# Spectrum and product buffer of a long-convolution kernel: four channels next to each other per frequency instead of two

## The chip, the cores and the metric

The kernel runs on one core of one Trainium2 chip. The metric is the time of one execution on the device, in microseconds (us); the time shown for a kernel is the median of its runs. Names of engines in the profile: PE is TensorE (matmuls), PEld its weight loads, DVE is VectorE, ACT is ScalarE, POOL is GpSimd, SP issues the DMAs. L90 is a line of a helper that records every operation, so nearly every row carries it and groups are told apart by their tiles.

## The reference

A long convolution per channel by FFT, and a gated projection behind it, for 8 batches of 6400 positions and 128 channels in fp32:

```python
def _attn_ref(x, h):                      # x: (8, 6400, 128), h: (6400, 128)
    L = 2 * S
    Yf = np.fft.rfft(x, n=L, axis=1) * np.fft.rfft(h, n=L, axis=0)[None]
    return np.fft.irfft(Yf, n=L, axis=1)[:, :S, :]

def _moe_ref(x, w_val, conv_w, w_out):    # x: what _attn_ref returned
    xp = np.concatenate([np.zeros((B, K - 1, D)), x], axis=1)
    gate_pre = sum(conv_w[k] * xp[:, k:k + S, :] for k in range(K))     # K = 5
    return (1 / (1 + np.exp(-gate_pre)) * (x @ w_val)) @ w_out
```

## The kernel before

The 6400 positions are laid out as N1 = 100 by N2 = 64, and the transforms are matmuls in steps. All data is fp32. The profile counts two PE instructions, and two weight loads, for each fp32 matmul of the code: a "pass" below is one of these two.

- **Forward step** (`Forward.group`): one group takes 8 channels. Four matmuls (weights: two channels of x, 128 columns; moving: the constants `r1_sb`, 200 columns) write a PSUM pair `pt`. Four copies bring it to the buffer `gy` (or to `gh`, a view of `dt`, for the filter h): 64 partitions by 400 elements each, on ACT in odd groups and on DVE in even groups.
- **Buffer `gy`**: per partition it holds, for each of the 128 channels, 100 frequencies. Before, the channels lie in pairs: `gy[p, d // 2, k, d % 2]`. Two channels of a pair are neighbours in memory (8 bytes together), the next frequency of the pair follows 8 bytes on, and the next pair 800 bytes on.
- **Second step** (`s2_mm`): for each frequency k one matmul with weights `m2_sb[:, k, :]` (128 dense columns) and, as moving operand, all 128 channels of that frequency, `src[:, :, k]`: 64 neighbouring pairs, 800 bytes apart. Eight frequencies fill a PSUM pair of two banks.
- **Product** (`Product`): the result is multiplied by the spectrum of h: `swap` (ACT, PSUM to `w_t`), `mul_u` (DVE, PSUM times `h_sb` into `gy`), `mul_t` (DVE, `w_t` times `h_sb`), `add` (POOL, into `gy`; DVE for the last block). `kdt` gives `w_t` and `h_sb` the same order of elements as `gy` has within a block of eight frequencies. `Spectrum` makes the spectrum of h once, at the start, and stores it to the scratch `hd` in device memory.
- **Third step** (`s3_quad`): for each channel one matmul with the channel's 100 frequencies as weights, `gy[:, d // 2, :, d % 2]` (100 columns, one every 8 bytes), and the constants `r3_sb` as moving operand (128 dense columns). Four channels fill one PSUM bank, which ACT or DVE copies to `dt`.
- **Fourth step and gates** (`Chunk`, `Gates`): `s4` (weights from `dt`, 128 dense columns; moving `m4_sb`, 100 columns), then taps, projection, sigmoid, gate, output projection, store.

The order of the work on every engine is the order of the code (`_InOrder`). Per batch there are two phases: first 16 rounds of two `s3_quad` and one `Forward.group` for the next batch (plus, from batch 1 on, the tail of the last batch's gates, `trail`); then the gates of this batch with the 13 `Product` blocks of the next batch between them. The first batch has a prologue in their place: 32 forward groups (16 for h, 16 for x), then spectrum and product blocks. The last batch has no forward groups and no products.

Of the kernel before, what the change touches and what calls it, by code (L numbers as in the profile page):

```python
# [9 lines left out]
F32 = mybir.dt.float32  # L10
# [5 lines left out]
C = 128  # L16
N1 = 100
N2 = 64
# [3 lines left out]
NKB = 13  # L22
TAPS = 5
XG = 8
NG = C // XG
NW = 2 * C + TAPS
SW = 256
# [75 lines left out]
def longconv_moe(ctx: ExitStack, tc: tile.TileContext, x, h, r1, m2, r3, m4, w64, out):  # L103
# [4 lines left out]
    cp = ctx.enter_context(tc.tile_pool(name="cp", bufs=1))  # L108
# [2 lines left out]
    psp = tc.tile_pool(name="psp", bufs=2, space=bass.MemoryType.PSUM)  # L111
    pairs = [ps2, psp.__enter__()]

    gy = cp.tile([128, C // 2, N1, 2], F32, name="gy")
    dt = cp.tile([128, N2 * 2 * C], F32, name="dt")
    dv = dt.rearrange("p (n c d) -> p n c d", c=2, d=C)
    gh = dt[:, : N1 * C].rearrange("p (d k t) -> p d k t", k=N1, t=2)
    m4_sb = cp.tile([PX, N2 + 1, N1], F32, name="m4_sb")
    r1_sb = cp.tile([N1, 2 * N1], F32, name="r1_sb")
    r3_sb = cp.tile([128, 2 * N2], F32, name="r3_sb")  # L120
# [5 lines left out]
    h_sb = [cp.tile([128, KB * C], F32, name=f"h_{i}") for i in range(HB)]  # L126
    x_sb = [cp.tile([PX, XG, N2], F32, name=f"x_{i}") for i in range(XB)]
    w_t = [cp.tile([128, KB * C], F32, name=f"w_{i}") for i in range(WB)]
# [66 lines left out]
    def pair():  # L195
        pairs.append(pairs.pop(0))
        return pairs[-1].tile([128, 2, 512], F32, name="pt2", tag="pt2")

    def single():
        return ps1.tile([128, 512], F32, name="pt1", tag="pt1")  # L200

    class Forward:
# [5 lines left out]
        def load(self, n=1):  # L208
            for _ in range(n):
                if self.n < NG:  # L210
                    nc.sync.dma_start(x_sb[self.n % XB], self.src[self.n])
                    self.n += 1

        def group(self):
            g = self.i
            self.i += 1
            t = x_sb[g % XB]
            pt = pair()
            for m in range(4):
                nc.tensor.matmul(  # L220
                    pt[:, m // 2, (m % 2) * SW : (m % 2) * SW + 2 * N1],
                    lhsT=t[:N1, 2 * m : 2 * m + 2, :].rearrange("p j n -> p (j n)"),
                    rhs=r1_sb,
                    start=True,
                    stop=True,
                )
            self.load()
            v = pt.rearrange("p b (m x) -> p b x m", x=SW)
            return [
                lambda e, j=j, c=c: e(  # L230
                    self.dst[c * N2 : (c + 1) * N2, 4 * g + 2 * j : 4 * g + 2 * j + 2],
                    v[j * N2 : (j + 1) * N2, :, c * N1 : (c + 1) * N1],
                )
                for j in range(2)
                for c in range(2)
            ]

    def count(kb):
        return min(KB, N1 - kb * KB)
# [6 lines left out]
    def h_load(kb):  # L246
        if kb < NKB:
            n = count(kb) * C
            for r in range(2):
                nc.sync.dma_start(h_sb[(2 * kb + r) % HB][:, :n], hd[kb, r, :, :n])  # L250
# [5 lines left out]

    def kdt(t, kb):
        n = count(kb)
        return t[:, : n * C].rearrange("p (d k t) -> p d k t", k=n, t=2)

    def s2_mm(src, kb):
        pt = pair()
        n = count(kb)
        for k in range(n):
            nc.tensor.matmul(
                pt[:, k // 4, (k % 4) * C : (k % 4 + 1) * C],
                lhsT=m2_sb[kb % M2B][:, k, :],
                rhs=src[:, :, kb * KB + k],
                start=True,
                stop=True,  # L270
            )
        if n <= 4:
            return pt[:, 0, : n * C].rearrange("p (k d t) -> p d k t", t=2, d=C // 2)
        return pt.rearrange("p b (k d t) -> p d (b k) t", t=2, d=C // 2)

    hx = h_sb + [dt[:, N1 * C + i * KB * C : N1 * C + (i + 1) * KB * C] for i in range(2)]

    class Spectrum:
        def __init__(self, kb):
            self.kb, self.v = kb, s2_mm(gh, kb)  # L280
            self.h = [hx[(2 * kb + r) % len(hx)] for r in range(2)]

        def real(self):
            t = kdt(self.h[0], self.kb)
            act(t[:N2], self.v[:N2])
            act(t[N2:], self.v[:N2])

        def imag(self):
            t = kdt(self.h[1], self.kb)
            dve(t[N2:], self.v[N2:])  # L290
            n = count(self.kb) * C
            nc.gpsimd.tensor_copy(self.h[1][:N2, :n], self.h[1][N2:, :n])
# [7 lines left out]
    class Product:  # L300
        def __init__(self, kb, h=None):
            self.kb, self.v = kb, s2_mm(gy, kb)
            self.t = kdt(w_t[kb % WB], kb)
            self.u = gy[:, :, kb * KB : kb * KB + count(kb)]
            self.h = [kdt(i, kb) for i in h or [h_sb[(2 * kb + r) % HB] for r in range(2)]]
# [15 lines left out]
    def s3_quad(d0):  # L321
        pt = single()
        for q in range(4):
            d = d0 + q
            nc.tensor.matmul(
                pt[:N1, q * 2 * N2 : (q + 1) * 2 * N2],
                lhsT=gy[:, d // 2, :, d % 2],
                rhs=r3_sb,
                start=True,
                stop=True,  # L330
            )
        o = dv[:N1, :, :, d0 : d0 + 4].rearrange("p n c d -> p (n c) d")
        return lambda e: e(o, pt[:N1].rearrange("p (d m) -> p m d", d=4))
# [129 lines left out]
    for f in (fh, fx):  # L463
        for g in range(NG):
            e = f.group()
            if f is fh and fh.n == NG:
                left = fx.n - (g + 1 - (NG - XB))
                if left < 0:
# [82 lines left out]
    for b in range(B):  # L551
# [5 lines left out]
        if nxt:  # L557
            for kb in range(M2B):
                m2_load(kb)
            for kb in range(2):  # L560
                h_load(kb)
        for g in range(NG):
            e = [s3_quad(8 * g), s3_quad(8 * g + 4)]
            f = fx.group() if nxt else []
            e[0](act)
            e[1](dve)
            for i in f:
                i(act if g % 2 else dve)
            if trail:
                trail.pop(0)()  # L570
            if b == 0:
                m4_load(4 * g, 4 * g + 4)
                if LATER + g < NKB:
                    h_double(LATER + g)
                next(wgen, None)
                next(wgen, None)
# [48 lines left out]
def _lay_x(v):  # L625
    b = v.shape[0]
    q = np.zeros((b, PX, C, N2), np.float32)
    q[:, :N1] = v.reshape(b, N1, N2, C).transpose(0, 1, 3, 2)
    q = q.reshape(b, PX, NG, 2, 4, N2).transpose(0, 2, 1, 4, 3, 5)
    return np.ascontiguousarray(q.reshape(b, NG, PX, XG, N2))  # L630

# [35 lines left out]
```

## Time and profile before

| | us |
|---|---|
| median of 3 runs (1089.99 to 1090.17) | 1090.0 |
| the profiled execution's own time | 1088.27 |
| span of the profiled execution, first to last instruction | 1086.5 |
| PE busy in the span | 1047.0 |
| DVE busy | 851.1 |
| ACT busy | 725.2 |
| POOL busy | 413.3 |

Busy time is a sum over phases with different limits, so the rows below are read by phase. The profiled execution's own time is 1.73 us below the median of the runs and 1.77 us above its span. A row of the timeline merges neighbouring instructions of one kind; its second number reaches to the end of the last one, and matmuls overlap, so the time that a run of matmuls takes from the engine is the start of the next row less the start of this one.

### The profile page before, as it was taken

To read this page: it belongs to the slowest core of one execution; us is meant where nothing else is said; L and a number is where in the kernel's file an instruction comes from. 1 tells how busy PE (TensorE), PEld (TensorE's weight loads), DVE (VectorE), ACT (ScalarE), POOL (GpSimd) and SP (SyncE) were. 2 spreads that over 40 slices of the span, in tenths; PEclk is the share of its full clock that TensorE was granted. 3 is DMA by queue.
4 is the path that set the end of the run, shared out by engine and by line. 5 is a ranking of instruction groups with operands and counts; after the bars stand their busy time and mean duration, and the time that the engine had idled before them with its cause. 6 is when DMAs were issued, how large, how long until landed. Compare 5 with 4: busy or idle time off the path is not lost.

```text
span 1086.5 us, 19537 instructions
## 1 busy us (share of the span) xinstructions
PE 1047.0 (96%) x7480; PEld 939.1 (86%) x7480; DVE 851.1 (78%) x1177; ACT 725.2 (67%) x1174; POOL 413.3 (38%) x219
## 2 busy tenths in 40 slices
PE   8997899999999999999999999999999999999997
PEld 8986899779988899878998799888998799987975
DVE  6789678987599857987589875998579885898375
ACT  5798348865588556875488656884578745885365
POOL 0079104840078202870058400881028600683032
PEclk9999899999999999999999999999999999999999
DMA  5697967975199734976279752997249761892012
GB/s 154 210 312 187 331 218 244 305 220 176 54 324 285 266 95 136 334 216 231 69 241 322 222 174 52 337 278 262 83 163 330 207 235 51 291 306 81 18 39 83
DMA packets 109130, 221.13 MB, mean 204 GB/s; under 512 B 45354, under 2 KB 53518, under 8 KB 108814
## 3 DMA queue, kind: packets, MB, share of 16 engines
q1 hardware_dynamic: 109038, 219.89, 63.1%
q8 instruction: 59, 0.97, 0.4%
q14 instruction: 33, 0.27, 0.1%
HBM read 184.47 MB, written 39.32 MB: 206 GB/s over the span
## 4 chain that ended last, share of the span: by engine, by line
PE 75%; ACT 13%; DVE 7%; DMA 2%; issue 2%; POOL 1%; POOLq 0%; SPq 0%; DVEq 0%; ACTq 0%
PE pt L90 75%; ACT w L90 6%; ACT dt L90 4%; DVE w L90 3%; DVE gl L90 2%; ACT p L90 2%; DMA x<-xl 1%; ACT h L90 1%; DVE gy L90 1%; DMA m<-m 1%; POOL gy L90 0%; DVE dt L90 0%; POOL dt L90 0%; ACT gl L90 0%; DMA x<-hl 0%
## 5 line engine op out<-in xcount | busy, mean ns | idle before, releaser
L90 PEld LDWEIGHTS pt<-m_sb,dt 100*128 100x128 f32 x2048 | 242.4, 192 | 43.4 <-issue 30.5
L90 PEld LDWEIGHTS pt<-r_sb,gy 128*100 128x100 f32 x2048 | 239.7, 172 | 31.8 <-issue 17.7
L90 ACT COPY dt<-pt 100x512 f32<-100x512 f32 (+3 forms) x280 | 163.4, 584 | 142.0 <-PE pt L90 140.5
L90 PE MATMUL pt<-r_sb,gy 128*100 128x128 f32 x2048 | 244.9, 274 | 10.5 <-DVE gy L90 10.5
L90 POOL TENSOR_TENSOR gy<-gy,w 128x1024 f32<-128x1024 f32 x96 | 228.5, 2380 | 58.2 <-DVE w L90 57.4
L90 PE MATMUL pt<-m_sb,dt 100*128 100x100 f32 x2048 | 243.7, 274 | 3.5 <-DVE dt L90 2.6
L90 PE MATMUL pt<-r_sb,x 100*128 100x200 f32 x1152 | 216.3, 335 | 6.1 <-DMA x<-hl 4.1
L90 PEld LDWEIGHTS pt<-gy,m 128*128 128x128 f32 x1600 | 194.5, 188 | 21.6 <-issue 9.9
L90 DVE COPY dt<-pt 100x512 f32<-100x512 f32 (+2 forms) x164 | 110.9, 679 | 120.3 <-PE pt L90 114.6
L90 PE MATMUL pt<-gy,m 128*128 128x128 f32 x1600 | 201.3, 278 | 1.1 <-DVE dt L90 1.1
L90 PEld LDWEIGHTS pt<-r_sb,x 100*128 100x128 f32 x1152 | 193.1, 192 | 6.7 <-issue 4.3
L90 ACT COPY gy<-pt 64x400 f32<-64x400 f32 x256 | 124.6, 487 | 100.9 <-PE pt L90 88.5
L90 DVE COPY gy<-pt 64x400 f32<-64x400 f32 x256 | 146.3, 571 | 37.6 <-PE pt L90 35.0
L90 POOL MEMSET dt<- 128x4 f32 x8 | 0.8, 106 | 456.9 <-PE pt L90 456.9
L90 DVE TENSOR_TENSOR w<-w,h 128x1024 f32<-128x1024 f32 (+1 forms) x100 | 150.4, 1504 | 0.0
L90 DVE SCALAR_TENSOR_TENSOR dt<-pt,w_sb,dt 128x500 f32<-128x500 f32 (+7 forms) x216 | 132.5, 629 | 12.7 <-POOL dt L90 6.1
L90 ACT ACTIVATE w<-pt 64x1024 f32<-64x1024 f32 (+1 forms) x104 | 102.8, 989 | 37.1 <-PE pt L90 35.6
L90 DVE TENSOR_TENSOR gy<-pt,h 128x1024 f32<-128x1024 f32 (+1 forms) x100 | 117.3, 1173 | 8.5 <-ACT w L90 4.9
L90 POOL TENSOR_TENSOR dt<-dt,p 128x500 f32<-128x500 f32 (+1 forms) x64 | 101.5, 1586 | 57.2 <-DVE dt L90 31.5
L90 PE MATMUL pt<-dt,w_sb 128*128 128x500 f32 (+2 forms) x240 | 114.0, 564 | 3.2 <-ACT dt L90 3.1
L90 DVE SCALAR_TENSOR_TENSOR gl<-pt,w_sb,gl 128x500 f32<-128x500 f32 (+3 forms) x119 | 73.9, 622 | 39.5 <-ACT gl L90 30.1
L90 ACT COPY w<-pt 64x1024 f32<-64x1024 f32 (+1 forms) x104 | 101.1, 972 | 1.5
(35 smaller groups left out, 722.7 us busy)
## 6 DMA issues: line engine op xcount, KB each, us to landing
h<-hd SPq DMA_DIRECT2D x168, 512.0 KB, 6.5
m<-m SPq DMA_DIRECT2D x96, 512.0 KB, 6.1
x<-xl SPq DMA_DIRECT2D x128, 224.0 KB, 3.4
out<-dt SPq DMA_DIRECT2D x56, 250.0 KB, 6.1
out<-yl SPq DMA_DIRECT2D x40, 250.0 KB, 2.8
hd<-h SPq DMA_DIRECT2D x8, 512.0 KB, 5.5
x<-hl SPq DMA_DIRECT2D x16, 224.0 KB, 2.6
hd<-hd SPq DMA_DIRECT2D x14, 256.0 KB, 5.2
```

Of the source, the lines that this page charges most:

```text
L90: return self._tc.keep_in_program_order(call(*args, **kwargs))
```

## The change

`TQ = 4` channels lie side by side per frequency in `gy` and `gh`, in the products' temporaries `w_t` and in the spectrum of h (`h_sb`, `hd`): `gy[p, d // 4, k, d % 4]`. Four channels are neighbours (16 bytes together), the next frequency of the four follows 16 bytes on, and the next four channels 1600 bytes on.

```diff
+TQ = 4
...
-    gy = cp.tile([128, C // 2, N1, 2], F32, name="gy")
+    gy = cp.tile([128, C // TQ, N1, TQ], F32, name="gy")
...
-    gh = dt[:, : N1 * C].rearrange("p (d k t) -> p d k t", k=N1, t=2)
+    gh = dt[:, : N1 * C].rearrange("p (d k t) -> p d k t", k=N1, t=TQ)
...
-                    self.dst[c * N2 : (c + 1) * N2, 4 * g + 2 * j : 4 * g + 2 * j + 2],
+                    self.dst[c * N2 : (c + 1) * N2, 2 * g + j].rearrange("p k (b m) -> p b k m", b=2),
                     v[j * N2 : (j + 1) * N2, :, c * N1 : (c + 1) * N1],
...
     def kdt(t, kb):
         n = count(kb)
-        return t[:, : n * C].rearrange("p (d k t) -> p d k t", k=n, t=2)
+        return t[:, : n * C].rearrange("p (d k t) -> p d k t", k=n, t=TQ)
...
         if n <= 4:
-            return pt[:, 0, : n * C].rearrange("p (k d t) -> p d k t", t=2, d=C // 2)
-        return pt.rearrange("p b (k d t) -> p d (b k) t", t=2, d=C // 2)
+            return pt[:, 0, : n * C].rearrange("p (k d t) -> p d k t", t=TQ, d=C // TQ)
+        return pt.rearrange("p b (k d t) -> p d (b k) t", t=TQ, d=C // TQ)
...
-                lhsT=gy[:, d // 2, :, d % 2],
+                lhsT=gy[:, d // TQ, :, d % TQ],
                 rhs=r3_sb,
```

No instruction is added, removed or moved on any engine, and the waits are the same; only the patterns of addresses differ. On DVE this shows at the end of the prologue's forward groups and at the first product. Before (64x400 is the copies' output of 64 partitions by 400 elements in one run, 128x64x16 that of `mul_u`):

```order
L90 COPY gy<-pt_401 64x400 x4
L90 COPY h_84<-pt_424 64x1024
L90 COPY h_86<-pt_433 64x1024
L90 TENSOR_TENSOR gy<-pt_448,h_83 128x64x16
L90 TENSOR_TENSOR w_91<-w_91,h_84 128x1024
```

The same rows of the changed kernel, whose lines stand one further down:

```order
L91 COPY gy<-pt_401 64x2x100x2 x4
L91 COPY h_84<-pt_424 64x1024
L91 COPY h_86<-pt_433 64x1024
L91 TENSOR_TENSOR gy<-pt_448,h_83 128x32x32
L91 TENSOR_TENSOR w_91<-w_91,h_84 128x1024
```

The copy into `gy` (and into `gh`) now writes pairs of elements, one pair every 16 bytes, where it wrote 400 elements in a row; `mul_u` and `add` touch `gy` in runs of 32 elements instead of 16; the other shapes stay.

## The prediction

> **What bounds the kernel now.** I read the page's engine shares and its chain first, then busy times by stage, then the chain of waits within one batch, then the timeline of PE for the pace of each kind of matmul.
>
> ```profile
> span 1086.5 us, 19537 instructions
> ...
> PE 1047.0 (96%) x7480; PEld 939.1 (86%) x7480; DVE 851.1 (78%) x1177; ACT 725.2 (67%) x1174; POOL 413.3 (38%) x219
> ...
> PE 75%; ACT 13%; DVE 7%; DMA 2%; issue 2%; POOL 1%; POOLq 0%; SPq 0%; DVEq 0%; ACTq 0%
> ```
>
> PE is busy 96% of the span and holds three quarters of the chain that ended last; ACT and DVE hold 20%. The windows tell where: the forward groups and the products of the prologue, then the two phases of the third batch.
>
> ```profile
> core 0: us, PE busy (x) PEld busy (x) DVE busy (x) ACT busy (x) POOL busy (x), PEclk, DMA share, GB/s
> 28.20:49.90 21.70, 21.70 (x128) 21.70 (x129) 17.85 (x32) 15.33 (x32) 0.00 (x0) 1.00 0.68 208
> 53.60:98.10 44.50, 41.23 (x346) 40.18 (x344) 40.82 (x31) 43.09 (x44) 37.02 (x19) 1.00 0.86 275
> ...
> 362.80:417.70 54.90, 54.77 (x398) 51.67 (x396) 37.19 (x60) 27.42 (x54) 0.00 (x0) 1.00 0.45 150
> 417.70:488.30 70.60, 69.77 (x498) 59.59 (x499) 63.32 (x79) 57.74 (x86) 49.30 (x25) 1.00 0.84 263
> ```
>
> In the third-step phase (362.8 to 417.7) PE is busy 54.77 of 54.90 us while DVE and ACT have 17.7 and 27.5 us to spare: PE alone is the limit there. In the gates phase PE is nearly as full, but there a busy PE is not always what is waited for. The chain of waits says where it is:
>
> ```profile
> 361.90 55.66 PE pt L90 x398
> 417.69 9.99 PE pt L90 x84
> 437.42 1.32 ACT dt L90 x4
> 441.83 1.65 ACT dt L90 x3
> 444.58 33.70 PE pt L90 x231
> 480.75 1.22 DVE w L90
> ```
>
> All of the third-step phase is PE (361.90 to 417.56). In the gates phase the first 9.99 us and 33.70 us from 444.58 on are PE's; between them ACT's copies and activations are the chain, and DVE takes the last 8 us.
>
> **What a pass costs PE.** The change alters how PE reads `gy` twice: as weights in the third step, as moving operand in the second. So I need the pace of each kind, from starts of neighbouring rows; the first row below is the group of the third step's weight loads, the others are of the timeline.
>
> ```profile
> L90 PEld LDWEIGHTS pt<-r_sb,gy 128*100 128x100 f32 x2048 | 239.7, 172 | 31.8 <-issue 17.7 <-POOL gy L90 10.6 <-DVE gl L90 1.4
> ...
> 118.25 1.91 PE L90 MATMUL pt<-r_sb,gy 128*100 128x128 f32 x16
> 120.00 1.52 PE L90 MATMUL pt<-r_sb,x 100*128 100x200 f32 x8
> 121.36 1.91 PE L90 MATMUL pt<-r_sb,gy 128*100 128x128 f32 x16
> ...
> 439.36 2.37 PE L90 MATMUL pt<-m_sb,dt 100*128 100x100 f32 x20
> 441.57 1.06 PE L90 MATMUL pt<-dt,w_sb 128*128 128x400 f32 x4
> ```
>
> A third-step pass takes (120.00 - 118.25) / 16 = 109.4 ns, a forward pass (121.36 - 120.00) / 8 = 170 ns, a fourth-step pass (441.57 - 439.36) / 20 = 110.5 ns. The first two move 128 and 200 dense columns: (170 - 109.4) / 72 = 0.84 ns a column and 2 ns beside it, so the moving columns set the pace, and the third step's 100 weights, one every 8 bytes, are loaded in its shade. The fourth step moves only 100 columns (86 ns by that rate) but loads 128 dense weights: there the load sets the pace, (110.5 - 2) / 128 = 0.85 ns a weight. Load and multiply run side by side, and the longer one counts. A load of 100 weights would take about 87 ns at that rate, so 22 ns of cover are left in a third-step pass.
>
> The second step:
>
> ```profile
> 55.47 2.02 PE L90 MATMUL pt<-dt,m 128*128 128x128 f32 x16
> 57.33 2.01 PE L90 MATMUL pt<-gy,m 128*128 128x128 f32 x16
> 59.18 2.01 PE L90 MATMUL pt<-dt,m 128*128 128x128 f32 x16
> ```
>
> (59.18 - 55.47) / 32 = 115.9 ns: 6.5 ns over the third step for the same 128 moving columns, 5.4 over the fourth step for the same 128 dense weights. What is special here is the moving operand: 64 pairs that lie 800 bytes apart. So a broken read costs PE something, and the two ways to write it down part ways for this change:
>
> - a **floor**: each new piece of memory takes at least 115.9 / 64 = 1.81 ns, however little of it is used;
> - a **charge**: each jump adds 6.5 / 64 = 0.10 ns.
>
> The third step's weights of today fit both, if a piece has at least 16 bytes: one weight every 8 bytes, two to a piece, 50 pieces of 1.81 ns are 91 ns, below 109.4.
>
> **The change part by part.**
>
> *Third step, weights.* Now one weight every 16 bytes: a piece of 16 bytes holds one. By the floor a load takes 100 x 1.81 = 181 ns, which is longer than the multiply, and the pace becomes 181 ns. By the charge it takes 87 + 100 x 0.10 = 97 ns, still hidden. No row of this trace has a PE read of one element per 16 bytes, so the price lies between: nothing (109.4 stays) and 181. I take 181: it comes from the only row in which PE reads broken data, and 16 bytes is the smallest piece that the rows allow; larger pieces (32 bytes) would again put two weights in each and cost nothing. By the Trainium skill (SBUF — State Buffer, Specifications) SBUF is read in lines of 16 bytes and at least two hits on a line are needed for full bandwidth. By that rule this change, which leaves one hit, slows the loads, and today's weights, with two, are just free; the trace agrees with the second half (109.4 ns), and no run here shows the first. [...]
>
> Sum: a round of the third-step phase has 16 third-step passes behind 8 forward passes. The load for a pass runs beside the pass before it. So the first load hides beside a forward pass (181 - 170 = 11 ns late) and 15 loads each make their pass 181 - 109.4 = 71.6 ns longer: 1.085 us a round. Seven batches of 16 rounds: 112 x 1.085 = 121.5 us. The last batch has no forward passes: 16 x 16 x 71.6 ns = 18.3 us. Together +139.8 us. All of it is on the path, by the chain of the phase above (55.66 us of PE without a break), and nothing else becomes late, since DVE and ACT had slack there already.
>
> *Second step, moving operand.* Now 32 pieces of 16 bytes: by the floor 58 ns, no limit any more. The pace falls to that of 128 dense weights, 110.5 ns: -5.4 ns a pass. What of it is on the path: in the gates phase those passes that lie in the two PE stretches of the chain.
>
> ```profile
> 419.63 3.95 PE L90 MATMUL pt<-gy,m 128*128 128x128 f32 x32
> ...
> 448.60 2.01 PE L90 MATMUL pt<-gy,m 128*128 128x128 f32 x16
> ...
> 477.40 1.08 PE L90 MATMUL pt<-gy,m 128*128 128x128 f32 x8
> ```
>
> The first stretch has 32 passes, the second five rows of 16 and one of 8 (first and last shown): 120 of the batch's 200. 7 x 120 x 5.4 ns = -4.5 us. The other 80 stand beside ACT's chain, and those of the prologue beside ACT too (43.09 of 44.50 us busy). At most, were all 1800 passes on the path, -9.7 us; at least 0, if the 6.5 ns come from loading and moving 128 columns at once and not from the jumps, a mixture that no row here has with a dense operand.
>
> *Copies of the forward groups.* They write pairs with a gap in place of one run.
>
> ```profile
> L90 DVE COPY gy<-pt 64x400 f32<-64x400 f32 x256 | 146.3, 571 | 37.6 <-PE pt L90 35.0
> L90 ACT COPY gy<-pt 64x400 f32<-64x400 f32 x256 | 124.6, 487 | 100.9 <-PE pt L90 88.5 <-DVE gl L90 10.1
> L90 DVE COPY dt<-pt 100x512 f32<-100x512 f32 x128 | 87.7, 689 | 109.5 <-PE pt L90 104.3 <-DMA m<-m 3.9
> ```
>
> The 512-element copy writes runs of four, 512 bytes apart, and costs (689 - 571) / 112 = 1.05 ns more per element, just as much as if both wrote dense runs. I take nothing for pairs, and a doubling (about 0.42 us a copy on DVE) as the other end. In the third-step phase even that hides (17.7 us to spare for 32 copies a batch on DVE, 13.4 us). In the prologue's forward groups DVE has four copies, 2.28 us, in two groups of PE, 2.71 us (16 passes of 170 ns): cover ends at 0.68 us a copy.
>
> *Products.* `mul_u`, `swap` and `add` keep their counts of elements, and their runs get longer.
>
> ```profile
> L90 POOL TENSOR_TENSOR gy<-gy,w 128x1024 f32<-128x1024 f32 x96 | 228.5, 2380 | 58.2 <-DVE w L90 57.4
> L90 DVE TENSOR_TENSOR gy<-pt,h 128x1024 f32<-128x1024 f32 x92 | 111.9, 1216 | 8.5 <-ACT w L90 4.9 <-DMA h<-hd 3.2
> L90 ACT COPY w<-pt 64x1024 f32<-64x1024 f32 x96 | 96.4, 1005 | 1.4
> ```
>
> Against the 400-element copies DVE's 1216 is (1216 - 571) / 624 = 1.03 ns an element, and ACT's 1005 is (1005 - 487) / 624 = 0.83: the rate of the other rows already, in spite of runs of two in PSUM. Nothing to win there, nothing to lose; POOL is far from the chain. The DMAs move the same blocks.
>
> *Sum.* +139.8 - 4.5 = +135.3 us. From the profiled execution's own 1088.27 us this is 1223.6; the median of the runs is 1.7 higher, so I say **1225 us**.
>
> **The rivals.**
>
> 1. *The weights' stride stays hidden* (a charge per jump, or pieces of 32 bytes). Speaks for it: the 22 ns of cover, and that the stride of 8 bytes is free today. It decides below a load of 109 ns, 1.07 ns a weight. Then only the second step is left: 1090 - 4.5 = 1085.5 us, between 1080 and 1090. The Trainium skill (SBUF — State Buffer, on cachelines) also says that fp32 may stride by 4 elements for free, which is this result if the stride of exactly 16 bytes is included; its own two-hits rule in the same passage says it is not. Chance 0.19, of it 0.15 for a gain over 0.2%.
> 2. *No effect at all*: weights hidden, and the 6.5 ns have nothing to do with the pairs. 1090 us. Chance 0.06.
> 3. *The copies become the bound of the prologue* while the weights stay hidden: at doubled copies, DVE needs 3.96 us per two groups against 2.71, 16 x 1.25 = +20 us, 1105 to 1110 us. Against it: dense and broken writes of the rows above run alike. Chance 0.02.
> 4. *A smaller price*: a load slower than its cover but below the floor. Each 10 ns over 109.4 give about 20 us: 1095 to 1195 us. Chance 0.06.
> 5. *A higher price*: the jump of one element costs more than that of a pair. At 2.6 ns a weight (half as much again as the floor) a pass takes 260 ns, +290 us, 1375. Nothing in the rows points there. Chance 0.04.
>
> **How the numbers follow.** The forecast with its own range of 1195 to 1245 us has 0.63: the low end is a load at twice the dense price, 2 x 0.85 x 100 = 170 ns, hence 112 x 15 x 60.6 + 256 x 60.6 ns = +117 us without and +113 with the second step's gain, 1203, and a little room; the high end is the floor plus 10 ns a pass. Cases of both signs hold much of the chance, so the range for 8 in 10 must reach to rival 1: 1083 to 1245 us. Left out are rival 5, the far end of rival 1 and some of the tails. A measurement of this kernel tells 0.2% (2.2 us) from no change: faster 0.15; same 0.10 (rival 2 and the rest of rival 1); slower 0.75.
>
> **What would show it.** In the changed kernel's timeline: third-step runs of 16 in about 2.85 us instead of 1.75, and their weight loads longer than the 172 ns of today by about 70; second-step runs of 16 in 1.77 instead of 1.85 us; third-step phases of 72 us instead of 55; copies of 571 and 487 ns as before. If third-step runs keep 1.75 us, the floor is wrong and rival 1 or 2 holds. If the runs lengthen but the phase does not, something else was the limit there.

## The result and the profile after

The changed kernel takes 1227.8 us (median of 4 runs, 1226.84 to 1228.37) against 1090.09 us before (1089.99 to 1093.09): ratio 1.1249, 95% interval 1.123 to 1.1268. The forecast was 1225.

The page of the changed kernel, the lines that answer to those of before:

```profile
span 1225.1 us, 19537 instructions
...
PE 1185.8 (97%) x7480; PEld 1085.8 (89%) x7480; DVE 852.7 (70%) x1177; ACT 733.5 (60%) x1174; POOL 412.5 (34%) x219
...
PE 82%; DVE 7%; ACT 7%; issue 2%; DMA 2%; POOL 0%; POOLq 0%; SPq 0%; DVEq 0%; ACTq 0%
```

The span grew by 138.6 us and PE's busy time by 138.8; DVE's and POOL's work is what it was, and ACT's grew by 8.3 us. The groups by shape (busy us, mean ns of one, idle before) say which matmuls; first the third and the second step's matmuls in the kernel before, then the rows of the changed kernel:

```profile
L90 PE MATMUL pt<-r_sb,gy 128*100 128x128 f32 x2048 | 244.9, 274 | 10.5 <-DVE gy L90 10.5
L90 PE MATMUL pt<-gy,m 128*128 128x128 f32 x1600 | 201.3, 278 | 1.1 <-DVE dt L90 1.1
```

```profile
L91 PEld LDWEIGHTS pt<-r_sb,gy 128*100 128x100 f32 x2048 | 390.4, 279 | 27.5 <-issue 13.5 <-POOL gy L91 10.7 <-DVE gl L91 0.2
L91 PE MATMUL pt<-r_sb,gy 128*100 128x128 f32 x2048 | 389.3, 344 | 10.5 <-DVE gy L91 10.5
...
L91 PE MATMUL pt<-gy,m 128*128 128x128 f32 x1600 | 196.5, 277 | 4.3 <-ACT gy L91 2.8 <-DVE dt L91 1.1 <-DVE gy L91 0.2
...
L91 DVE COPY gy<-pt 64x400 f32<-64x400 f32 x256 | 146.6, 573 | 44.3 <-PE pt L91 41.7
L91 ACT COPY gy<-pt 64x400 f32<-64x400 f32 x256 | 132.4, 517 | 133.2 <-PE pt L91 131.0
```

The third step's weight load went from 172 to 279 ns, and the time in which PE was busy with the third step by 144.4 us (244.9 to 389.3); the second step gained 4.8 (201.3 to 196.5). The timeline gives the pace; starts are in the first column.

```profile
454.02 3.05 PE L91 MATMUL pt<-r_sb,gy 128*100 128x128 f32 x16
456.91 1.52 PE L91 MATMUL pt<-r_sb,x 100*128 100x200 f32 x8
458.26 3.05 PE L91 MATMUL pt<-r_sb,gy 128*100 128x128 f32 x16
```

A run of 16 third-step passes takes 2.89 us (before 1.75), a round 4.24 us (before 3.11). If the first load of a run hides beside the forward pass ahead of it, as the prediction has it, only 15 of the 16 passes wait for their load: (2.89 - 0.11) / 15 = 185 ns a pass. In windows, the third-step phase and the gates phase of the third batch:

```profile
397.60:470.90 73.30, 73.30 (x398) 70.89 (x399) 37.79 (x60) 28.39 (x54) 0.00 (x0) 1.00 0.34 112
470.90:540.60 69.70, 68.20 (x498) 58.47 (x496) 63.31 (x79) 57.47 (x86) 49.17 (x25) 1.00 0.83 266
```

PE is busy without a break for all of the first, and its weight loads for 70.89 of 73.30 us. By the starts of rows in both timelines, from a batch's first third-step pass to the PE row behind its last one, and from there to the next batch's first:

| us | before | after | difference |
|---|---|---|---|
| prologue, to the first third-step pass | 113.0 | 114.0 | +1.0 |
| third-step phases, 8 together | 407.0 | 547.2 | +140.2 |
| gates phases, 7 together | 507.4 | 504.8 | -2.6 |
| the end, after the last third-step phase | 59.0 | 59.0 | 0 |

The loss lies in the third-step phases. The prologue's +1.0 cannot be read as an effect: two of the kernels below differ from before in the third step's weights alone, which the prologue does not use, and theirs lasts 110.9 us (weights dense) and 114.2 us (every 12 bytes).

### The profile page after: what moved, and what is told of

It reads as the page before. It is cut to its first block, busy times and chain, and to the rows that moved or that the text cites. A ratio compares the mean times of both kernels' runs of the same rounds, so it can differ in the third digit from the quotient of the medians.

```text
span 1225.1 us, 19537 instructions
## 1 busy us (share of the span) xinstructions
PE 1185.8 (97%) x7480; PEld 1085.8 (89%) x7480; DVE 852.7 (70%) x1177; ACT 733.5 (60%) x1174; POOL 412.5 (34%) x219
## 4 chain that ended last, share of the span: by engine, by line
PE 82%; DVE 7%; ACT 7%; issue 2%; DMA 2%; POOL 0%; POOLq 0%; SPq 0%; DVEq 0%; ACTq 0%
PE pt L91 82%; DVE w L91 3%; ACT w L91 3%; ACT dt L91 2%; DVE gl L91 2%; DVE gy L91 1%; DMA h<-hd 1%; ACT p L91 1%; ACT gy L91 1%; DMA m<-m 1%; DVE dt L91 1%; POOL dt L91 0%; DVE h L91 0%; DMA x<-hl 0%; POOL gy L91 0%
## 5 line engine op out<-in xcount | busy, mean ns | idle before, releaser
L91 PEld LDWEIGHTS pt<-r_sb,gy 128*100 128x100 f32 x2048 | 390.4, 279 | 27.5 <-issue 13.5
L91 PE MATMUL pt<-r_sb,gy 128*100 128x128 f32 x2048 | 389.3, 344 | 10.5 <-DVE gy L91 10.5
L91 POOL TENSOR_TENSOR gy<-gy,w 128x1024 f32<-128x1024 f32 x96 | 227.7, 2372 | 60.9 <-DVE w L91 60.1
L91 PEld LDWEIGHTS pt<-gy,m 128*128 128x128 f32 x1600 | 190.3, 192 | 25.8 <-issue 10.1
L91 ACT COPY gy<-pt 64x400 f32<-64x400 f32 x256 | 132.4, 517 | 133.2 <-PE pt L91 131.0
L91 PE MATMUL pt<-gy,m 128*128 128x128 f32 x1600 | 196.5, 277 | 4.3 <-ACT gy L91 2.8
L91 PEld LDWEIGHTS pt<-r_sb,x 100*128 100x128 f32 x1152 | 196.9, 195 | 4.3 <-issue 4.3
```

The lines of the kernel that those rows point to most:

```text
L91: return self._tc.keep_in_program_order(call(*args, **kwargs))
```

## The experiments

The theory: a weight load needs about 1.80 ns for each 16-byte piece of memory that it touches, and with one weight in each piece the load, not the multiply, sets the third step's pace. Rivals: the loss needs the four-wide copies, products or second step; or the price goes by something else than 16-byte pieces (any step over 8 bytes, distance, a charge per jump). In the first four, `gf` is `gy` with its free dimensions in one row of 12,800 elements.

**Four wide everywhere, weights every 8 bytes.** The third step reads the addresses of the old pairs, so its weights are not the right channels.

```diff
-                lhsT=gy[:, d // TQ, :, d % TQ],
+                lhsT=gf[:, (d // 2) * 2 * N1 + d % 2 : (d // 2 + 1) * 2 * N1 : 2],
```

> The changed kernel, but the third step reads its weights every 8 bytes (within the old pairs' addresses, so they are not the right channels); the second step's reads, the copies and the products stay four wide. Theory (the whole loss is the third step's weight load, 1.80 ns for each 16-byte piece that it touches): third-step runs of 16 passes fall from 2.89 back to 1.75 us, and the time to 1085 to 1090 us. Rival (part of the loss is in the copies, in new waits or in the products): the runs fall, but the time stays above 1095 us.

1087.76 us beside 1091.15 for before, ratio 0.996 (0.9944 to 0.9977). Timeline:

```profile
412.43 1.91 PE L91 MATMUL pt<-r_sb,gy 128*100 128x128 f32 x16
414.18 1.52 PE L91 MATMUL pt<-r_sb,x 100*128 100x200 f32 x8
```

Runs of 16 are back at 1.75 us, and with them the whole loss is gone: copies, products and the spectrum's four-wide form cost nothing that shows in the time. What stays is a gain of 0.4%, 2.5 to 6.1 us by the interval. Of it, 2.6 us lie where the second step is: the gates phases last 504.8 us together, as in the changed kernel, against 507.4 before.

**The same, copies dense.** As above, and the forward copies fill their block of 400 elements in a row (values land on other frequencies).

```diff
-  self.dst[c * N2 : (c + 1) * N2, 2 * g + j].rearrange("p k (b m) -> p b k m", b=2),
+  self.dst[c * N2 : (c + 1) * N2, 2 * g + j].rearrange("p k t -> p (k t)").rearrange("p (b k m) -> p b k m", b=2, m=2),
```

> As the kernel with four-wide layout and weights every 8 bytes, and the copies of the forward groups write 400 elements in a row again (to the right block, in another order, so the values land on other frequencies). Theory: ACT's copy falls from 517 back to 487 ns, DVE's stays at 572; the time is that of the former kernel within 2 us, since ACT waits for PE there. Rival (the first wait of the second step for the last copy costs the gain of the second step): 2 us or more below the former kernel, 1085 to 1087 us.

1087.35 us, ratio to before 0.9954 (0.9937 to 0.997). ACT's copy is at 487 ns again, so writing pairs with gaps is what costs it 30 ns; the time of the two kernels cannot be told apart. That is the theory's side: the broken writes are hidden. What they cost the second step is small: in the traces the gates phases last 504.3 us together with dense copies and 504.8 without, a difference below what the times tell.

**Pairs as before, weights every 16 bytes.** The reverse: only the third step's reads are changed.

```diff
-                lhsT=gy[:, d // 2, :, d % 2],
+                lhsT=gf[:, d0 * N1 + q : (d0 + 4) * N1 : 4],
```

> The kernel before with pairs everywhere, but the third step reads its weights every 16 bytes (within its four channels, mixed values). Theory: third-step pace 184 ns as in the changed kernel, time 1226 to 1233 us. Rival (the loss needs the four-wide second step, copies or products): below 1220 us.

1230.23 us, ratio to before 1.1263 (1.1236 to 1.129). In the timeline a run takes 447.14 - 444.25 = 2.89 us, that of the changed kernel:

```profile
444.25 3.05 PE L90 MATMUL pt<-r_sb,gy 128*100 128x128 f32 x16
447.14 1.52 PE L90 MATMUL pt<-r_sb,x 100*128 100x200 f32 x8
```

With the first experiment this settles it: the stride of the weights is enough for the loss, and without it there is none.

**Pairs, weights dense, every 12 bytes and every 32 bytes.** Three kernels, each with another slice of the same block:

```diff
+                lhsT=gf[:, d * N1 : (d + 1) * N1],                                     # dense
+                lhsT=gf[:, d0 * N1 + q : d0 * N1 + q + 3 * N1 - 2 : 3],                # 12 bytes
+                lhsT=gf[:, d // 8 * 8 * N1 + d % 8 : (d // 8 + 1) * 8 * N1 : 8],       # 32 bytes
```

> The kernel before, but the third step reads 100 neighbouring elements as weights (mixed frequencies and channels of the right block). Theory (pieces of 16 bytes with a floor of 1.80 ns): 25 pieces, no limit; runs of 16 stay at 1.75 us and the time at 1090 us within 2; the weight load's own duration stays near 172 ns. Rival (a charge for each jump): the load gets shorter by up to 10 ns, still hidden, the same time.

> The kernel before, the third step's weights one every 12 bytes (within its four channels, mixed values). 100 weights lie in 75 pieces of 16 bytes. Theory (floor of 1.80 ns per 16-byte piece): 75 x 1.80 + 4.5 = 139.5 ns a pass, 30 more than before, hence 112 x 15 x 30 + 256 x 30 ns = +58 us, 1148 us (1140 to 1155). Rival (every step of more than 8 bytes pays the full price per weight): 184 ns a pass, 1228 us. Rival (no price below 16 bytes): 109 ns, 1090 us.

> The kernel before, the third step's weights one every 32 bytes (within the eight channels of the round, mixed values). Theory (floor per touched 16-byte piece, wherever it lies): 100 pieces as at 16 bytes, 184 ns a pass, 1226 to 1233 us. Rival (the price rises with the distance, or pieces are larger than 16 bytes): clearly more than 184 ns, 1250 us or more.

Dense: 1090.66 us, ratio 0.9997 (0.9981 to 1.0014). Every 12 bytes: 1140.41 us, one run, beside 1089.9 for before; every 32 bytes: 1234.66, also one run, 1.7 us above the range expected. The first two rows are of the timeline with 12 bytes, the last two of that with 32; the weight loads' groups follow for dense, 12 and 32 bytes:

```profile
427.63 2.33 PE L90 MATMUL pt<-r_sb,gy 128*100 128x128 f32 x16
429.80 1.52 PE L90 MATMUL pt<-r_sb,x 100*128 100x200 f32 x8
```

```profile
442.57 3.09 PE L90 MATMUL pt<-r_sb,gy 128*100 128x128 f32 x16
445.49 1.52 PE L90 MATMUL pt<-r_sb,x 100*128 100x200 f32 x8
```

```profile
L90 PEld LDWEIGHTS pt<-r_sb,gy 128*100 128x100 f32 x2048 | 238.9, 168 | 31.8 <-issue 17.7 <-POOL h L90 7.3 <-POOL gy L90 3.0
```

```profile
L90 PEld LDWEIGHTS pt<-r_sb,gy 128*100 128x100 f32 x2048 | 297.9, 224 | 29.7 <-issue 14.8 <-POOL gy L90 10.7 <-ACT gl L90 0.2
```

```profile
L90 PEld LDWEIGHTS pt<-r_sb,gy 128*100 128x100 f32 x2048 | 395.4, 281 | 27.3 <-issue 13.6 <-POOL gy L90 10.7
```

| weights every | 16-byte pieces per load | run of 16, us | a pass, (run - 0.11) / 15, ns | mean load, ns |
|---|---|---|---|---|
| 4 bytes | 25 | 1.75 | 109 | 168 |
| 8 bytes (before) | 50 | 1.75 | 109 | 172 |
| 12 bytes | 75 | 2.17 | 137 | 224 |
| 16 bytes (changed) | 100 | 2.89 | 185 | 279 |
| 32 bytes | 100 | 2.92 | 187 | 281 |

From 75 to 100 pieces the pace grows by 48 ns, 1.9 ns a piece; from 100 pieces at 16 bytes to 100 at 32 by only 2. So neither the distance nor "any step over 8 bytes" sets the price, but the number of 16-byte pieces, and the first 50 of them hide behind the multiply. Pieces of another size don't fit the table: with pieces of 8 bytes, a step of 8, 12 or 16 bytes would cost the same; with pieces of 32, a step of 32 would cost about twice one of 16. The dense kernel decides nothing between floor and charge: its load became 4 ns shorter in the record (172 to 168), and the time is the same by both. With 12 bytes the time was forecast at 1148 and came to 1140, the low end of the range: the pass is 2.5 ns shorter than 139.5, and the rest of the difference has no experiment.

**One wide.** The same code with `TQ = 1`: the third step's weights are dense, the second step moves 128 single elements, the copies write single elements.

```diff
-TQ = 4
+TQ = 1
...
-  self.dst[c * N2 : (c + 1) * N2, 2 * g + j].rearrange("p k (b m) -> p b k m", b=2),
+  self.dst[c * N2 : (c + 1) * N2, 8 * g + 4 * j : 8 * g + 4 * j + 4, :, 0].rearrange("p (b m) k -> p b k m", b=2),
```

> The layout with one channel per frequency (weights of the third step dense, the second step's moving operand 128 single elements, 400 bytes apart; the copies write single elements). Theory (the floor holds for the moving operand and for writes too): 128 x 1.80 = 231 ns a second-step pass instead of 115.5, third step at 109.4; the products' phases get 200 x 115.5 ns = 23 us longer in each of 7 batches and the prologue's by about 43 us, and with copies of about 0.87 us on DVE another 13 us in the prologue's forward groups: 1290 to 1310 us. Rival (a charge of 0.10 ns per jump): 122 ns a pass, 1095 to 1105 us.

1315.21 us, one run. The timeline, then the copies' groups:

```profile
67.44 3.81 PE L91 MATMUL pt<-gy,m 128*128 128x128 f32 x16
71.07 3.88 PE L91 MATMUL pt<-dt,m 128*128 128x128 f32 x16
```

```profile
L91 ACT COPY gy<-pt 64x400 f32<-64x400 f32 x256 | 222.0, 867 | 93.6 <-PE pt L91 91.1
L91 DVE COPY gy<-pt 64x400 f32<-64x400 f32 x256 | 220.9, 863 | 29.7 <-PE pt L91 26.7
```

A second-step pass takes (71.07 - 67.44) / 16 = 227 ns, 1.77 ns for each of 128 pieces: the same floor on the moving operand, against 115.9 for pairs. A charge of 0.10 ns per jump is out. Copies that write 400 single elements cost 863 and 867 ns on two engines whose dense copies differ (571 and 487): (867 - 487) / 400 is 0.95 ns more an element on ACT, which had 0.83, so 1.78 in all; DVE had 1.05, now (863 - 571) / 400 = 0.73 more, 1.78 as well. The time lies 5 us over the range expected: the gates phases became 22.5 us longer each, near the 23 forecast, and the prologue 46 us (56 forecast), but six third-step phases also grew, to 57.2 us each from 53.2 to 55.2, where nothing was expected. In the second of the eight phases the chain of waits runs over DVE from 306.94 to 328.06 us, through copies into `gy` of about 0.87 us and, between them, the tail of the previous batch's gates, and PE waits 2.0 us for those gates. So the slower copies stand in the chain there; that they alone cause the growth was not tried by itself.

**Four wide, buffer shifted by 8 bytes.** Is it runs of neighbours that count, or pieces at fixed addresses?

```diff
-    gy = cp.tile([128, C // TQ, N1, TQ], F32, name="gy")
+    gf = cp.tile([128, C * N1 + 4], F32, name="gy")
+    gy = gf[:, 2 : C * N1 + 2].rearrange("p (d k t) -> p d k t", k=N1, t=TQ)
```

> The changed kernel, the product buffer moved up by 8 bytes, so that each four channels of a frequency lie across a 16-byte boundary (if the buffer starts on one); the spectrum's buffer is not moved. Theory (the floor counts aligned 16-byte pieces): the second step's passes on the product buffer touch 64 pieces again, 115.5 ns a pass; those on the spectrum's buffer stay at 111.5; the third step stays at 184 ns, time 1226 to 1233 us. Rival (the floor counts runs of neighbours, whatever their address): both kinds at 111.5 ns.

1228.06 us, one run, beside 1093.42 for before. Timeline of the prologue:

```profile
57.89 1.99 PE L91 MATMUL pt<-gy,m 128*128 128x128 f32 x16
59.72 1.95 PE L91 MATMUL pt<-dt,m 128*128 128x128 f32 x16
61.50 1.99 PE L91 MATMUL pt<-gy,m 128*128 128x128 f32 x16
```

On the shifted buffer a pass takes (59.72 - 57.89) / 16 = 114.4 ns, on the other (61.50 - 59.72) / 16 = 111.3. The shift alone takes back most of what four neighbours had won (111.6 to 114.4 of 115.9), so the address matters and not only the run; that it falls 1.5 ns short of the pairs' 115.9 is not explained.

## Why the prediction was right

- **PE alone bounds the third-step phase**: right. PE and the chain stayed full there (73.30 of 73.30 us), and all the loss is in these phases.
- **The floor, 181 ns a pass**: right; measured 185. In the record the load itself became 107 ns longer (172 to 279), where the prediction gave about 70 as its sign: at a pace of 185 ns, loads recorded with 279 ns overlap, so their length is not the pace. The step between floor and charge, which the rows of before left open, was decided for the floor by five strides of the weights and by the one-wide layout. The Trainium skill's rule (SBUF — State Buffer, Specifications: at least two hits on a 16-byte line for full bandwidth) agrees with these runs: two weights per piece at 109 ns, one at 185. A step of exactly four fp32 elements, which rival 1 took for free, costs 76 ns a pass here.
- **+1.085 us a round, 139.8 us in all**: the round grew by 1.13 us, more than forecast, and the eight phases by 140.2 together. That the sums lie within 0.4 us is in part luck, for the parts differ more: six phases grew by 17.6 to 17.9 us where 17.4 was forecast, the last by 17.3 where 18.3 was, and the fourth only from 55.2 to 71.1, since before it had held a wait of PE for a load of x (1.70 us by its row) that no longer shows.
- **Second step, 110.5 ns**: right in kind; (57.91 - 54.34) / 32 = 111.6 ns in the changed kernel (rows below). **-4.5 us on the path** was too much: the gates phases gave 2.6. A pass gained 4.3 and not 5.4 ns, and 2600 / (7 x 4.3) is the gain of 86 of 200 passes a batch, where I had counted 120. In the third batch the second PE stretch, with 88 passes, shrank from 33.70 to 33.42 us, which is 0.28 of the phase's 0.38 and less than 88 x 4.3 ns; the 32 passes of the first stretch brought next to nothing, and the first of them now waits 0.41 us for ACT's last copy, as its row shows.

```profile
54.34 1.95 PE L91 MATMUL pt<-gy,m 128*128 128x128 f32 x16
56.13 1.95 PE L91 MATMUL pt<-dt,m 128*128 128x128 f32 x16
57.91 1.95 PE L91 MATMUL pt<-gy,m 128*128 128x128 f32 x16
...
473.32 3.84 PE L91 MATMUL pt<-gy,m 128*128 128x128 f32 x32 [0.41 <-ACT gy L91]
```

- **Copies cost nothing**: right for DVE (573 against 571 ns), wrong for ACT (517 against 487), and without effect on the time that these runs can tell. The floor would give the 30 ns: 200 pairs at 1.8 ns are 360 ns, where ACT's dense rate needs 400 x 0.83 = 332; DVE, at 1.05 ns an element, takes longer than the floor anyway.
- **Products and POOL unchanged**: right (1217 and 2372 ns against 1216 and 2380).
- **Rival 1** would have been the result with weights every 8 bytes: that kernel came out 3.4 us below the kernel before (1087.76 against 1091.15), where the rival said 4.5.

No version that beats the kernel before came out of this. The gain of the second step wants more than two channels of one frequency in a piece, the third step wants two frequencies of one channel, and a piece holds four elements. All three ways to split a piece were run: four frequencies of one channel (one wide, 1315.21 us), two by two (before, 1090.09) and four channels of one frequency (the change, 1227.8). Only pairs leave both steps near their limits; layouts other than these were not tried.

## What to carry to other kernels

A buffer that one matmul reads along one index and another along a different one should be judged by how many 16-byte pieces each read touches: pieces x 1.8 ns against the time that hides it. That is the time that the engine needs for the elements anyway (0.85 ns each on PE in fp32 here), and for a weight load also the multiply beside it (109 ns here). Below that, strides were free in these kernels, as the pairs' stride of 8 bytes was (50 pieces, 90 ns); above it, the read became the bound, and a weight load that had been invisible under its multiply set the pace. Look for the cover in the trace of before, and for any row in which the same engine already reads broken data: here 64 pieces in 115.9 ns, only 6.5 ns over a dense read, gave the price of a change of 138 us.

## What the runs showed of the hardware

The price per piece came out as nearly one number on three engines: 1.77 ns for PE's moving operand, 1.78 for single-element writes of both ACT and DVE, and between 1.8 and 1.9 for weight loads. Reads of PSUM did not show it: the dense copies of 487 and 571 ns read single elements of PSUM 1 KB apart.

In the kernel shifted by 8 bytes POOL's addition became faster, with the same shape and work; its row, after which 2015 ns stand against 2372 in the changed kernel:

```profile
L91 POOL TENSOR_TENSOR gy<-gy,w 128x1024 f32<-128x1024 f32 x96 | 193.5, 2015 | 71.8 <-DVE w L91 61.7 <-PE pt L91 8.8 <-ACT w L91 1.3
```

Why is open; POOL holds 0% of the chain in that kernel, and the time did not move (1228.06 us against 1227.8).
